# Top-32 attention and a gated product on one core: the values of two slots made together in every second turn

## The chip, the cores and the metric

One Trainium2 chip, one of its NeuronCores. The metric is the device time of one execution in microseconds (us); the median of the runs shown stands for a kernel. TensorE is PE in the profile (PEld is its weight loading), VectorE is DVE, ScalarE is ACT, GpSimd is POOL, SyncE is SP.

## The reference

```python
batch, n_heads, seq, head_dim = (8, 8, 576, 64)
scores = scale * np.matmul(q, k.transpose(0, 1, 3, 2))
kth = np.partition(scores, -top_k, axis=-1)[..., -top_k:-top_k + 1]      # top_k = 32
scores = np.where(scores >= kth, scores, -1000000000.0)
attn = np.exp(scores - np.max(scores, axis=-1, keepdims=True))
attn = attn / (np.sum(attn, axis=-1, keepdims=True) + 1e-09)
x = np.matmul(attn, v)                   # then heads side by side: 4608 tokens x 512
a = x @ w1; b = x @ w2                   # 512 -> 1024
h = a * b @ w3                           # 1024 -> 1024
out = h @ w_out                          # 1024 -> 512
```

All data is float32.

## The kernel before, in words

**Slots.** The attention is cut into 144 slots, 18 for each of 8 batches. A slot holds 128 query rows of two heads (or 64 rows of four heads, `t == 4`) against all 576 keys. Ten slots make part 0 of a batch (320 tokens), eight make part 1 (256 tokens). When a part's last slot is done, its dense product (`moe_steps`: eight pairs of `ab` sums, then four `eo` sums, each a chain of 12 or 24 matmuls) joins a queue. `w3` and `w_out` are folded into one weight `wf` at the start, where all weights are also decoded and split into a high and a low part.

**Turns.** The loop over `p` (lines 575 to 646) is a pipeline written out by hand; every engine keeps the program's order (`InOrder`). In one turn, and in this order, four neighbouring slots are at work: DVE makes the 32 largest scores of slot `p` (`top32_steps`, tiles `w` and `top`, given out in pieces by `next(finder)`); ACT and POOL make mask and exponentials of slot `p - 1` (`mask`, `exps`, `invert`, `normalise`); PE turns the weights of slot `m = p - 2` (`turn`: eight transposes of 128 columns into the PSUM tile `tp`, a ninth, of the last keys of both heads, into `ro`), ACT copies them to SBUF (`take_turned`: `pts`, `pr`); PE makes the scores of slot `p + 1` (`scores`: tiles `st`), and then, with `pts` and `pr`, the values of slot `m` (`values`: 20 matmul records, two heads at a time in the two column halves, into columns 128 to 255 of `ro`). ACT takes the high part of the values (`take_high`), DVE the low part in the next turn (`take_low`, tile `xf`), between its first two passes over the scores `w<-s,st` and its next two `w<-w,st`.

**Filling.** Between these steps PE takes matmuls from the queue of dense products: `fill(SHARE[0])` before the transposes, `fill(SHARE[1])` before the scores, `fill(SHARE[2])` after the values. The shares are constants. `fill` first evicts sums that are complete (ACT copies, a DVE product `whole`, a POOL subtraction).

**PSUM.** Pool `ps_a` has two buffers of two banks, which `st` (twice a turn) and `tp` (once) take by turns. So `tp` waits until DVE's passes `w<-s,st` have read the buffer of the first `st` tile, and the second `st` tile waits until ACT has copied `tp`. `ro` has one buffer, the `ab` and `eo` sums have three.

**SBUF.** Pool `x` (line 82) has nine buffers for `xf` and for the weights `y` under decoding; `pts` has one buffer, `pr` two.

Of the kernel before, what the change touches and what calls it, by code (L numbers as in the profile page):

```python
# [9 lines left out]
F32 = mybir.dt.float32  # L10
# [52 lines left out]
def attn_moe(ctx: ExitStack, tc: tile.TileContext, q, k, v, w1, w2, w3, w_out, out, flag, general):  # L63
# [12 lines left out]
    pe, act, dve, pool, sp = nc.tensor, nc.scalar, nc.vector, nc.gpsimd, nc.sync  # L76
# [2 lines left out]
    kq_p = ctx.enter_context(tc.tile_pool(name="kq", bufs=AHEAD))  # L79
    att_p = ctx.enter_context(tc.tile_pool(name="att", bufs=2))  # L80
    small = ctx.enter_context(tc.tile_pool(name="small", bufs=4))
    x_p = ctx.enter_context(tc.tile_pool(name="x", bufs=9))
    g_p = ctx.enter_context(tc.tile_pool(name="g", bufs=4))
    z_p = ctx.enter_context(tc.tile_pool(name="z", bufs=4))
    o_p = ctx.enter_context(tc.tile_pool(name="o", bufs=2))
# [1 line left out]
    ps_v = ctx.enter_context(tc.tile_pool(name="ps_v", bufs=1, space=PSUM))  # L87
    ps_m = ctx.enter_context(tc.tile_pool(name="ps_m", bufs=3, space=PSUM))

    ident = const.tile([128, 128], F32, name="ident")  # L90
# [17 lines left out]
    if not general:  # L108
        pe, act, dve, pool, sp = (InOrder(tc, e) for e in (pe, act, dve, pool, sp))
# [239 lines left out]
        for a in range(2):  # L349
            pool.tensor_scalar(pab[:, a, :], pab[:, a, :], sums[:, a : a + 1], 1.0, op0=ALU.mult, op1=ALU.mult)  # L350

    def turn(pab):

        tp = ps_a.tile([128, 2, 512], F32, tag="a", name="tp")
        flat = pab[:].rearrange("p a c -> p (a c)")
        for a in range(2):
            for c in range(4):
                o = a * (S + 64) + c * 128
                pe.transpose(tp[:, a, c * 128 : (c + 1) * 128], flat[:, o : o + 128], ident)
        ro = ps_v.tile([128, 512], F32, tag="v", name="ro")  # L360
        pe.transpose(ro[:, :128], flat[:, 512:640], ident)
        return tp, ro

    def take_turned(tp, ro):
        pts = att_p.tile([128, 2, 512], F32, tag="pts", name="pts", bufs=1)
        act.copy(pts, tp)
        pr = att_p.tile([128, 128], F32, tag="pr", name="pr")
        act.copy(pr, ro[:, :128])
        return pts, pr

    def values(vts, t, pts, pr, ro):

        ov = ro[:, 128:256]
        ends = t == 4
        for j in range(2 if ends else 1):
            vt = vts[j]
            for c in range(5):
                for i, h in enumerate(HEADS):
                    block = i * 4 + c if c < 4 else (((8, 10), (10, 9))[j][i] if ends else 8 + i)
                    n = HEADS[i ^ j] if ends else slice(0, 128)  # L380
                    rhs = pr[:, n] if c == 4 else pts[:, j if ends else i, c * 128 + n.start : c * 128 + n.stop]
                    to = ov[h, j * 64 : j * 64 + 64] if ends else ov[h]
                    pe.matmul(to, vt[:, block * D : (block + 1) * D], rhs, start=(c == 0), stop=(c == 4))
        return ov

    def places(xs, t):
        o = PLACE[t]
        if t == 4:
            return [(x, slice(o, o + 64), slice(j * 64, j * 64 + 64)) for j, x in enumerate(xs)]
        return [(xs[0], slice(o, o + 128), slice(0, 128))]  # L390

    def take_high(to, ov):
        for x, cols, n in to:
            act.copy(x[:, 0, cols], ov[:, n])

    def take_low(to, ov):
        for x, cols, n in to:
            dve.tensor_tensor(x[:, 1, cols], ov[:, n], x[:, 0, cols].bitcast(F32), op=ALU.subtract)
# [75 lines left out]
    def new_x():  # L474
        return x_p.tile([128, 2, NA], F32R, tag="x", name="xf")

    if general:
        for src, step in startup:
            for _ in step(fetch(src), False):
                pass  # L480
        with tc.For_i(0, B, 1) as b:
            seen = small.tile([1, 1], I32, tag="seen", name="seen", bufs=1)
            nc.sync.dma_start(seen, flag[ds(b + 1, 1), :])
            with tc.If(nc.values_load(seen, min_val=0, max_val=1) > 0):
                for part in range(2):
                    qk, vts, xs = {}, {}, {}
                    for of, hps, t in SLOTS:
                        if of != part:
                            continue
                        for hp in hps:  # L490
                            if hp not in qk:
                                qk[hp], vts[hp], xs[hp] = load_qk(b, part, hp), load_v(b, hp), new_x()
                        s, st = new_s(), scores([qk[hp] for hp in hps], t)
                        for h in range(2):
                            take_scores(s, st, h)
                        edge = top32_exact(s)
                        pab, sums = new_weights()
                        for a in range(2):
                            mask(s, edge, pab, a)
                            exps(edge, pab, sums, a)  # L500
                        enlarge(sums)
                        invert(sums)
                        normalise(pab, sums)
                        tp, ro = turn(pab)
                        ov = values([vts[hp] for hp in hps], t, *take_turned(tp, ro), ro)
                        to = places([xs[hp] for hp in hps], t)
                        take_high(to, ov)
                        take_low(to, ov)
                    for _ in moe_steps(b, part, [xs[hp] for hp in range(NHP)], lambda f: f()):
                        pass  # L510
        return
# [6 lines left out]
    queue = []  # L518

    parted = [u for u in units if u[0] > 0]  # L520
    put_off = []
    spare = 0

    def evict():
# [46 lines left out]
    n_slots = len(slots)  # L571
    for p in range(-1, n_slots + 3):
        i, j, m = p + 1, p - 1, p - 2
        if i < n_slots:
            for u in units:
                if first[u] - 2 == i:
                    qk[u] = load_qk(*u)
                if first[u] == i:
                    vts[u] = load_v(u[0], u[2])
        finder = top32_steps(ss[p], *sts.pop(p), p) if 0 <= p < n_slots else iter(())  # L580
        if 0 <= j < n_slots:
            edges[j] = edges_of(j)
        next(finder, None)
        for u in parted:
            if first[u] - 1 == i:
                split_k(PARTS[u[1]][1], qk[u])
        for u in parted:
            if first[u] - 1 == i:
                rest_k(PARTS[u[1]][1], qk[u])
        for u in parted:  # L590
            if first[u] - 0 == i:
                rest_q(PARTS[u[1]][1], qk[u])
        if m - 1 in lows:
            take_low(*lows.pop(m - 1))
            b, part, _ = slots[m - 1][0][0]
            if final[b, part] == m - 1:
                queue.append(moe_steps(b, part, [xts.pop((b, part, hp)) for hp in range(NHP)], put_off.append))
        next(finder, None)
        if p >= 0:
            warm()  # L600
        if 0 <= j < n_slots:
            pabs[j] = new_weights()
            for a in range(2):
                mask(ss[j], edges[j], pabs[j][0], a)
            compare(j)
        for u in parted:
            if first[u] - 1 == i:
                split_q(PARTS[u[1]][1], qk[u])
        fill(SHARE[0])
        next(finder, None)  # L610
        if 0 <= m < n_slots:
            tp, ro = turn(pabs[m][0])
            pts, pr = take_turned(tp, ro)
        warm(False)
        if 0 <= j < n_slots:
            exps(edges[j], *pabs[j], 0)
            exps(edges[j], *pabs[j], 1)
            enlarge(pabs[j][1])
        weigh(2)
        fill(SHARE[1])  # L620
        next(finder, None)
        warm(False)
        if i < n_slots:
            st = scores([qk[u] for u in slots[i][0]], slots[i][1])
            ss[i] = new_s()
            take_scores(ss[i], st, 0)
            sts[i] = st, take_scores(ss[i], st, 1)
        if 0 <= m < n_slots:
            us, t = slots[m]
            for u in us:  # L630
                if u not in xts:
                    xts[u] = new_x()
            ov = values([vts[u] for u in us], t, pts, pr, ro)
            lows[m] = places([xts[u] for u in us], t), ov
            take_high(*lows[m])
        next(finder, None)
        warm()
        next(finder, None)
        if 0 <= j < n_slots:
            invert(pabs[j][1])  # L640
            normalise(*pabs[j])
        weigh(8)
        fill(SHARE[2])
        for _ in finder:
            pass
        if 0 <= m < n_slots:
            del ss[m], pabs[m], edges[m]
        warm()
# [62 lines left out]
```

## Time and profile before

| | |
|---|---|
| runs | 1230.25, 1230.30, 1231.37 us; median 1230.3 us |
| the profiled execution | 1230.32 us, of which the span from first to last instruction is 1228.5 us |
| busy over the span | PE 97%, PEld 87%, DVE 92%, ACT 81%, POOL 81% |
| granted TensorE clock | 0.994 over the span |
| chain that ended last | PE 88%, DVE 7%, ACT 2% |

All work is recorded under one line (L54, the helper that keeps the order), so rows are told apart by their tiles. In a row of the timeline stand the start, the time from the first start to the last end, the engine, the operation, the output and input tiles, the shape, how many instructions are merged, and in brackets the idle time before with its releaser. A float32 matmul has two records.

### The profile page before, as it was taken

What the parts mean: (1) busy time and instruction counts of PE and PEld (TensorE: products, weight loads), DVE (VectorE), ACT (ScalarE), POOL (GpSimd) and SP (SyncE); (2) the same over time, 40 slices, a digit from 0 to 9 for tenths busy, and PEclk for the clock granted to TensorE, in tenths of its full rate; (3) what the DMA queues carried; (4) which work ended last, traced back from release to release, by engine and by line L of the source; (5) the groups of instructions that cost most, each with busy time, mean ns of one, the idle gap of its engine ahead of it and who ended that gap; (6) DMA issues with size and microseconds to landing.
All of it is one profiled execution on the core that took longest, in us unless ns stands there. A gap on an engine that the chain in (4) does not pass through costs nothing.

```text
span 1228.5 us, 31126 instructions
## 1 busy us (share of the span) xinstructions
PE 1189.1 (97%) x10967; PEld 1070.4 (87%) x10967; DVE 1133.9 (92%) x3960; ACT 998.2 (81%) x2140; POOL 996.5 (81%) x1331
## 2 busy tenths in 40 slices
PE   4799799999999999999999999999999999999998
PEld 2454589999999999999999999999999999999998
DVE  7999999999999999999999999999999999999910
ACT  6888888888888888888888888888888888888731
POOL 6998978888978888888888888888888888888721
PEclk9899999999999999999999999999999999999999
DMA  6544411213121211213121121203111120202000
GB/s 232 178 170 157 157 57 40 67 33 96 41 67 55 71 59 35 72 33 96 41 68 55 47 83 34 73 28 98 43 59 63 41 78 29 89 28 80 6 22 21
DMA packets 42807, 85.98 MB, mean 70 GB/s; under 512 B 4754, under 2 KB 21138, under 8 KB 42642
## 3 DMA queue, kind: packets, MB, share of 16 engines
q1 hardware_dynamic: 42642, 83.91, 21.2%
q8 instruction: 88, 1.44, 0.5%
q14 instruction: 77, 0.63, 0.2%
HBM read 74.45 MB, written 9.44 MB: 68 GB/s over the span
## 4 chain that ended last, share of the span: by engine, by line
PE 88%; DVE 7%; ACT 2%; issue 1%; POOL 1%; DMA 0%; SPq 0%; DVEq 0%; ACTq 0%; POOLq 0%
PE ab L54 33%; PE eo L54 17%; PE ro L54 15%; PE st L54 12%; PE tp L54 10%; DVE w L54 3%; DVE top L54 2%; PE pf L54 2%; DVE y L54 1%; DVE wl L54 1%; POOL pab L54 0%; ACT t L54 0%; ACT pab L54 0%; POOL wo L54 0%; ACT s L54 0%
## 5 line engine op out<-in xcount | busy, mean ns | idle before, releaser
L54 DVE MAX8 top<-w 128x8 f32<-128x192 f32 (+1 forms) x1152 | 477.9, 447 | 0.0
L54 PE MATMUL ab<-xf,wh 128*128 128x256 f32 (+1 forms) x2048 | 439.2, 303 | 4.9 <-DVE y L54 2.4
L54 POOL TENSOR_TENSOR pab<-s,pab 128x576 f32<-128x576 f32 x288 | 406.9, 1435 | 25.8 <-ACT pab L54 24.0
L54 PEld LDWEIGHTS ab<-xf,wh 128*128 128x128 f32 x2048 | 334.2, 189 | 15.8 <-issue 9.2
L54 PE MATMUL ab<-xf,wl 128*128 128x256 f32 (+1 forms) x1024 | 308.2, 301 | 0.0
L54 ACT ACTIVATE pab<-s,edge 128x576 f32<-128x576 f32 x288 | 208.0, 770 | 105.7 <-POOL edge L54 104.9
L54 DVE MATCH_REPLACE8 w<-top,w 128x192 f32<-128x192 f32 x864 | 289.3, 342 | 0.0
L54 POOL TENSOR_SCALAR pab<-pab,sums 128x576 f32<-128x576 f32 x288 | 211.6, 747 | 40.8 <-DVE sums L54 40.5
L54 ACT ACTIVATE pab<-pab,edge 128x576 f32<-128x576 f32 x288 | 223.9, 781 | 21.5 <-POOL pab L54 18.6
L54 PE MATMUL eo<-g,wf 128*128 128x256 f32 (+1 forms) x1536 | 231.5, 301 | 0.0
L54 PEld LDWEIGHTS eo<-g,wf 128*128 128x128 f32 x1536 | 208.3, 188 | 8.1 <-issue 7.5
L54 PEld LDWEIGHTS ab<-xf,wl 128*128 128x128 f32 x1024 | 193.5, 189 | 4.2 <-issue 4.2
L54 ACT COPY pts<-tp 128x1024 f32<-128x1024 f32 x144 | 145.7, 1012 | 42.9 <-PE tp L54 40.1
L54 ACT COPY s<-st 128x768 f32<-128x768 f32 (+1 forms) x288 | 169.5, 643 | 4.1 <-PE st L54 4.1
L54 DVE TENSOR_TENSOR w<-s,st 128x384 f32<-128x384 f32 x288 | 146.7, 551 | 21.5 <-ACT s L54 7.2
L54 DVE TENSOR_TENSOR w<-w,st 128x384 f32<-128x384 f32 x288 | 158.3, 550 | 4.9
L54 PE MATMUL ro<-pts,vt 128*64 128x128 f32 (+1 forms) x2560 | 160.4, 268 | 0.9 <-ACT pr L54 0.9
L54 PE MATMUL tp<-ident,pab 128*128 128x128 f32 x1152 | 150.6, 274 | 9.2 <-POOL pab L54 7.2
L54 PEld LDWEIGHTS tp<-ident,pab 128*128 128x128 f32 x1152 | 133.2, 141 | 15.8 <-POOL pab L54 8.4
L54 PEld LDWEIGHTS ro<-pts,vt 128*64 128x64 f32 x2560 | 126.8, 137 | 20.0 <-issue 4.2
L54 POOL TENSOR_TENSOR g<-whole,g 128x256 fp32r<-128x256 f32 (+1 forms) x128 | 103.5, 808 | 36.3 <-ACT g L54 32.6
L54 POOL TENSOR_SCALAR sums<-sums 128x2 f32<-128x2 f32 x144 | 30.8, 214 | 104.4 <-ACT pab L54 102.4
(64 smaller groups left out, 1572.8 us busy)
## 6 DMA issues: line engine op xcount, KB each, us to landing
vt<-in_v SPq DMA_DIRECT2D x64, 352.0 KB, 3.1
kt<-in_k SPq DMA_DIRECT2D x64, 320.0 KB, 3.9
z<-in_w SPq DMA_DIRECT2D x32, 512.0 KB, 3.5
qt<-in_q SPq DMA_DIRECT2D x32, 160.0 KB, 3.0
out_t<-osb SPq DMA_DIRECT2D x32, 160.0 KB, 1.8
z<-in_wo SPq DMA_DIRECT2D x8, 512.0 KB, 5.3
qt<-in_q SPq DMA_DIRECT2D x32, 128.0 KB, 3.0
out_t<-osb SPq DMA_DIRECT2D x32, 128.0 KB, 1.7
```

Source lines behind the costliest of these rows:

```text
L54: ins = fn(*args, **kw)
```

## The change

`turn` no longer makes its own `ro`: the loop makes one in turns with even `m`, whose transposes go to columns 0 to 127 and values to columns 128 to 255; the slot of the next turn uses columns 256 to 511 of the same tile. The turned weights of the even slot are held (`held`, so `pts` gets a second buffer), and in the odd turn the values of both slots are made one after the other, then both high parts are taken. The low parts of both are taken in the turn after that. The pool `x` goes from nine to eight buffers. Part ends fall on odd `m` (slots 9 and 17 of 18), so a part joins the queue in the same turn as before.

```diff
-    x_p = ctx.enter_context(tc.tile_pool(name="x", bufs=9))
+    x_p = ctx.enter_context(tc.tile_pool(name="x", bufs=8))
-    def turn(pab):
+    def turn(pab, ro, lane):
...
-        ro = ps_v.tile([128, 512], F32, tag="v", name="ro")
-        pe.transpose(ro[:, :128], flat[:, 512:640], ident)
-        return tp, ro
+        pe.transpose(ro[:, lane : lane + 128], flat[:, 512:640], ident)
+        return tp
-    def take_turned(tp, ro):
-        pts = att_p.tile([128, 2, 512], F32, tag="pts", name="pts", bufs=1)
+    def take_turned(tp, ro, o):
+        pts = att_p.tile([128, 2, 512], F32, tag="pts", name="pts")
...
-        if m - 1 in lows:
-            take_low(*lows.pop(m - 1))
+        for n in list(lows):
+            take_low(*lows.pop(n))
...
-            tp, ro = turn(pabs[m][0])
-            pts, pr = take_turned(tp, ro)
+            o = m % 2 * 256
+            if not o:
+                ro = new_ro()
+            held.append((m, *take_turned(turn(pabs[m][0], ro, o), ro, o), ro, o))
...
-        if 0 <= m < n_slots:
-            us, t = slots[m]
-            for u in us:
-                if u not in xts:
-                    xts[u] = new_x()
-            ov = values([vts[u] for u in us], t, pts, pr, ro)
-            lows[m] = places([xts[u] for u in us], t), ov
-            take_high(*lows[m])
+        if 0 <= m < n_slots and m % 2:
+            for n, *turned in held:
+                us, t = slots[n]
+                for u in us:
+                    if u not in xts:
+                        xts[u] = new_x()
+                lows[n] = places([xts[u] for u in us], t), values([vts[u] for u in us], t, *turned)
+            for n, *_ in held:
+                take_high(*lows[n])
+            held.clear()
```

The order of PE's instructions before, in one turn of the steady part, from the last scores to the next matmuls of the queue (`vt` are the values' rows, `pts` and `pr` the turned weights; the other turn of the pair reads the same with other numbers):

```order
L54 MATMUL st_8779<-hi_8458,lo_8459 128x192 x2
L54 MATMUL st_8779<-lo_8459,hi_8458 128x192 x2
L54 MATMUL ro_8744<-pts_8746,vt_8326 64x128 x8
L54 MATMUL ro_8744<-pr_8748,vt_8326 64x128 x2
L54 MATMUL ab_8762<-xf_7243,wl11_1532 128x320
L54 MATMUL ab_8762<-xf_7644,wh1_104 128x320 x2
```

The same place of the changed kernel in the even turn of the pair:

```order
L54 MATMUL st_8745<-hi_8424,lo_8425 128x192 x2
L54 MATMUL st_8745<-lo_8425,hi_8424 128x192 x2
L54 MATMUL ab_8728<-xf_7335,wl11_1515 128x320
L54 MATMUL ab_8728<-xf_7612,wh1_104 128x320 x2
L54 MATMUL ab_8728<-xf_7612,wl11_1515 128x320
```

and in the odd turn:

```order
L54 MATMUL st_8856<-hi_8669,lo_8670 128x192 x2
L54 MATMUL st_8856<-lo_8670,hi_8669 128x192 x2
L54 MATMUL ro_8701<-pts_8712,vt_8282 64x128 x8
L54 MATMUL ro_8701<-pr_8714,vt_8282 64x128 x2
L54 MATMUL ro_8701<-pts_8826,vt_8282 64x128 x8
L54 MATMUL ro_8701<-pr_8828,vt_8282 64x128 x2
L54 MATMUL ab_8834<-xf_7874,wh1_104 128x320
```

The ten matmuls of the values have left the even turn and stand behind the ten of the odd turn; the matmuls of the queue stay where they were.

DVE's order before, at the start of a turn's selection (`xf` is the low part of one slot):

```order
L54 TENSOR_TENSOR w_8947<-s_8911,st_8897 128x2x192 x2
L54 TENSOR_TENSOR xf_8789<-ro_8872,xf_8789 128x128
L54 TENSOR_TENSOR w_8947<-w_8947,st_8904 128x2x192 x2
L54 TENSOR_TENSOR whole_8965<-ab_8882,asb_8817 128x320
L54 MAX top0_100<-w_8947 128x8 x2
```

and after, in an even turn:

```order
L54 TENSOR_TENSOR w_8911<-s_8863,st_8849 128x2x192 x2
L54 TENSOR_TENSOR xf_8866<-ro_8701,xf_8866 128x128 x2
L54 TENSOR_TENSOR w_8911<-w_8911,st_8856 128x2x192 x2
L54 TENSOR_TENSOR whole_8930<-ab_8834,asb_8771 128x320
L54 MAX top0_100<-w_8911 128x8 x2
```

Both low parts stand in the even turn, and none in the odd one.

## Rows read from the trace of the kernel before

**Rows 1.** Stretches: length, busy us of PE, PEld, DVE, ACT, POOL; clock, DMA, GB/s.

```profile
0.00:168.85 168.85, 135.83 (x786) 81.80 (x787) 156.40 (x459) 139.12 (x271) 146.80 (x183) 0.96 0.49 168
...
569.88:709.13 139.25, 139.25 (x1364) 130.49 (x1364) 135.46 (x487) 117.64 (x257) 116.99 (x159) 1.00 0.19 58
...
1158.00:1228.50 70.50, 64.11 (x527) 62.60 (x525) 14.59 (x48) 22.18 (x54) 19.80 (x28) 0.99 0.06 19
```

**Rows 2.** Waits in 569.88 to 709.13: who for whom, us, times, longest.

```profile
DVE sums L54 <- POOL sums L54: 0.7, 2, 0.5
...
DVE w L54 <- ACT g L54: 0.5, 1, 0.5
```

**Rows 3.** Timeline of PE around one slot's values; the two x6 rows from narrower windows.

```profile
606.77 0.27 PE L54 MATMUL st<-hi,lo 64*128 64x192 f32 x2
606.88 0.27 PE L54 MATMUL st<-lo,hi 64*128 64x192 f32 x2
607.08 1.09 PE L54 MATMUL ro<-pts,vt 128*64 128x128 f32 x16
...
607.24 0.50 PE L54 MATMUL ro<-pts,vt 128*64 128x128 f32 x6
...
607.46 0.50 PE L54 MATMUL ro<-pts,vt 128*64 128x128 f32 x6
...
608.33 0.42 PE L54 MATMUL ab<-xf,wh 128*128 128x320 f32 x1
608.58 0.31 PE L54 MATMUL ab<-xf,wl 128*128 128x320 f32 x1
608.73 0.31 PE L54 MATMUL ab<-xf,wh 128*128 128x320 f32 x1
```

**Rows 4.** Timeline of DVE, turn 74 and the start of turn 75.

```profile
624.89 0.56 DVE L54 TENSOR_TENSOR w<-s,st 128x384 f32<-128x384 f32 x1
...
631.27 0.14 DVE L54 RECIPROCAL sums<-sums 128x2 f32<-128x2 f32 x1
...
633.11 0.28 DVE L54 TENSOR_TENSOR xf<-ro,xf 128x128 fp32r<-128x128 f32 x1
633.31 0.54 DVE L54 TENSOR_TENSOR w<-w,st 128x384 f32<-128x384 f32 x1
```

**Rows 5.** Timeline of PE, POOL and DVE in turn 75.

```profile
634.47 0.38 PE L54 MATMUL tp<-ident,pab 128*128 128x128 f32 x2
...
638.43 0.21 POOL L54 TENSOR_SCALAR sums<-sums 128x2 f32<-128x2 f32 x1 [0.84 <-ACT pab L54]
...
638.67 0.17 DVE L54 RECIPROCAL sums<-sums 128x2 f32<-128x2 f32 x1
```

**Rows 6.** Timeline of DVE and PE in turn 5, during loading.

```profile
58.39 1.00 DVE L54 TENSOR_TENSOR w<-s,st 128x384 f32<-128x384 f32 x2
...
59.53 0.85 PE L54 MATMUL tp<-ident,pab 128*128 128x128 f32 x6 [1.62 <-DVE w L54]
```

**Rows 7.** Timeline of DVE and PE: starts of turns 67, 69, 73 and 75.

```profile
569.88 0.56 DVE L54 TENSOR_TENSOR w<-s,st 128x384 f32<-128x384 f32 x1
...
572.65 1.03 PE L54 MATMUL tp<-ident,pab 128*128 128x128 f32 x8
...
586.43 0.55 DVE L54 TENSOR_TENSOR w<-s,st 128x384 f32<-128x384 f32 x1
...
617.60 1.02 DVE L54 TENSOR_TENSOR w<-s,st 128x384 f32<-128x384 f32 x2
...
618.93 1.03 PE L54 MATMUL tp<-ident,pab 128*128 128x128 f32 x8
...
632.17 1.02 DVE L54 TENSOR_TENSOR w<-s,st 128x384 f32<-128x384 f32 x2
```

**Rows 8.** Timeline of PE and POOL during loading.

```profile
118.08 1.98 PE L54 MATMUL pf<-wo,y 128*128 128x512 f32 x4
...
120.24 1.26 POOL L54 TENSOR_SCALAR y<-z 128x512 f32<-128x512 f32 x2
```

More of the change, by code (lines that the diff above doesn't have):

```diff
@@ L359, in turn, with new_ro, values @@
                 pe.transpose(tp[:, a, c * 128 : (c + 1) * 128], flat[:, o : o + 128], ident)
-        ro = ps_v.tile([128, 512], F32, tag="v", name="ro")
-        pe.transpose(ro[:, :128], flat[:, 512:640], ident)
-        return tp, ro
-    def take_turned(tp, ro):
-        pts = att_p.tile([128, 2, 512], F32, tag="pts", name="pts", bufs=1)
+        pe.transpose(ro[:, lane : lane + 128], flat[:, 512:640], ident)
+        return tp
+    def new_ro():
+        return ps_v.tile([128, 512], F32, tag="v", name="ro")
+    def take_turned(tp, ro, o):
+        pts = att_p.tile([128, 2, 512], F32, tag="pts", name="pts")
         act.copy(pts, tp)
         pr = att_p.tile([128, 128], F32, tag="pr", name="pr")
-        act.copy(pr, ro[:, :128])
+        act.copy(pr, ro[:, o : o + 128])
         return pts, pr
-    def values(vts, t, pts, pr, ro):
-        ov = ro[:, 128:256]
+    def values(vts, t, pts, pr, ro, o):
+        ov = ro[:, o + 128 : o + 256]
         ends = t == 4
@@ L503, in attn_moe @@
                         normalise(pab, sums)
-                        tp, ro = turn(pab)
-                        ov = values([vts[hp] for hp in hps], t, *take_turned(tp, ro), ro)
+                        ro = new_ro()
+                        ov = values([vts[hp] for hp in hps], t, *take_turned(turn(pab, ro, 0), ro, 0), ro, 0)
                         to = places([xs[hp] for hp in hps], t)
@@ L520, in attn_moe @@
     parted = [u for u in units if u[0] > 0]
-    put_off = []
+    put_off, held = [], []
     spare = 0
@@ L592, in attn_moe @@
                 rest_q(PARTS[u[1]][1], qk[u])
-        if m - 1 in lows:
-            take_low(*lows.pop(m - 1))
-            b, part, _ = slots[m - 1][0][0]
-            if final[b, part] == m - 1:
+        for n in list(lows):
+            take_low(*lows.pop(n))
+            b, part, _ = slots[n][0][0]
+            if final[b, part] == n:
                 queue.append(moe_steps(b, part, [xts.pop((b, part, hp)) for hp in range(NHP)], put_off.append))
@@ L611, in attn_moe @@
         if 0 <= m < n_slots:
-            tp, ro = turn(pabs[m][0])
-            pts, pr = take_turned(tp, ro)
+            o = m % 2 * 256
+            if not o:
+                ro = new_ro()
+            held.append((m, *take_turned(turn(pabs[m][0], ro, o), ro, o), ro, o))
         warm(False)
```

## The prediction

> **What bounds the kernel.** I read the busy time by stretch first, then the waits of the steady part, then the timelines of PE and DVE within a turn. In the 18 turns of one batch [rows 1] PE is busy for all of 139.25 us, and no wait of PE on another engine is in that stretch, so PE sets the pace: 7.74 us a turn, 15.47 for two. DVE is close behind: 135.5 us busy, and of what is left only 1.2 us are waits, for POOL's `sums` and once for ACT [rows 2]. The rest stands between its instructions in every turn. So DVE cannot turn 18 slots in less than about 139.25 - 1.2 = 138.05. Two engines with under 1% between them share this loop, and what matters is how far one may run ahead of the other. While weights load (0 to 169 us) DVE is busy 156 of 169 us and PE only 136 [rows 1]; after 1158 us the last part's products run on PE alone. The steady part in between holds 128 turns (989 us / 7.74), that is 7.1 batches.
>
> **The values move.** Around one slot's values [rows 3] the last scores start at 606.88 and the second matmul of the queue at 608.58: 1.70 us. Scores run in pairs 0.11 apart (606.77 to 606.88). The values too: the two narrow windows begin two pairs apart, at 607.24 and 607.46, so ten pairs take 1.09. Queue matmuls of this width are 0.15 apart (608.58 to 608.73). 1.70 - 0.11 - 1.09 - 0.15 leaves 0.35 lost where the kind of matmul changes: about 0.15 from scores to values (607.08 instead of 606.99, the next pair 0.16 later) and 0.20 from values to queue (608.33, then 0.25 instead of 0.15).
>
> An even turn now goes from scores straight to the queue, which no row of before shows. Such a change costs between 0 and the whole 0.35; I take 0.20, as from values to queue, which is the same step back to full-width matmuls. The even turn then needs 0.11 + 0.20 + 0.15 = 0.46 in place of 1.70, so it is 1.24 shorter; the odd turn makes ten more pairs with no change between them, 1.09 longer. PE gains 0.15 in two turns: 15.32 for 15.47, and 137.9 for 139.25 in a batch (bounds: 139.25 at 0.35, 136.1 at nothing). If PE stayed the bound, 64 pairs x 0.15 = 9.6 us would go. The rule for this: the Trainium skill, "TensorEngine Tiling (Array Packing)", section Key Properties, says that changing the tiling mode, and not just the tile, drains TensorE. The 0.35 in [rows 3] agrees; by that rule alone the time would be 1230.3 - 9.6 = 1220.7.
>
> **What the values' place does to PE's lead.** Every turn PE's transposes `tp` take the PSUM buffer that DVE's `w<-s,st` must first have read. When PE has to wait for that, `tp` starts 1.14 us after `w<-s,st` (58.39 to 59.53, [rows 6]). That is the earliest place. There is a latest one too, past which DVE pays: from `tp` the work goes over ACT's copy and exponentials and POOL's `sums` to DVE's reciprocal, 4.20 us (634.47 to 638.67, with the `sums` at 638.43, [rows 5]). Undisturbed, the reciprocal comes 6.38 after `w<-s,st` (624.89 to 631.27, [rows 4]), so `tp` may start up to 2.18 after it before DVE waits, some 0.4 more in turns where a `whole` product stands ahead of the reciprocal. The room is 1.0 to 1.5 us.
>
> Before, all of it is in use already: `tp` stands 2.77 after `w<-s,st` in turn 67 (569.88, 572.65) and 1.33 in turn 73 (617.60, 618.93) [rows 7], because DVE's pairs of turns are uneven (16.55 us from 569.88 to 586.43, 14.57 from 617.60 to 632.17: the `whole` products come in clusters) while PE's are even. PE never hits the early end; DVE hits the late one for the 1.2 us of [rows 2].
>
> After, the place also swings within each pair. From the `tp` of an odd turn to that of the even turn lie both values: 1.09 more for PE, and DVE's odd turn is 0.2 shorter, since its low part (633.11 to 633.31, [rows 4]) has moved to the even one: `tp` is 1.3 later. On the way back PE is 1.24 less and DVE 0.2 more: 1.4 earlier. This swing alone fills the room, and nothing is left for the drift of 1.44. In odd turns PE stands before `tp` until DVE has read the scores; in even turns DVE's reciprocal comes late. PE can no longer gain on one pair what DVE gives up in another, so each pair takes the longer of the two. With PE's 15.32 and DVE's nine pairs of this batch less their waits (from 14.6 to 16.0 us; of the nine, [rows 7] has the shortest and the longest, which also holds 0.7 of waits) the sum of the larger is 139.8. That is a lower bound of this case, since it still lets each pair use its room freely. On top, in odd turns the reciprocal is due 0.2 sooner while the chain through mask and exponentials does not move: 0 to 0.2 in nine turns, 0 to 1.8. Most odd turns that have a `whole` first keep their slack, so I take 0.3: **140.1 us a batch**, 0.85 more than before.
>
> **The rest.** ACT and DVE do the same copies; `pts` has its second buffer, so holding it delays nothing. The high parts come in pairs at the end of an odd turn, where ACT next waits for POOL's `edge` anyway. No DMA and no queue of SP or POOL is moved. Loading is bound by DVE, and the end has only one slot's pair in it: 0, give or take 2 us.
>
> **Sum.** 7.1 x 0.85 = +6.0 on the profiled 1230.32 us (span 1228.5 and 1.8 around it), which is the median of the runs too: **1236.3 us**.
>
> **Rivals.**
> - *PE keeps its lead (faster).* If the room is wider than I read it, by a microsecond or so, both engines run free, and the larger floor decides: DVE's 138.05 against PE's 137.9, so 1.2 a batch, 8.5 us: 1221.8. For it: the 2.77 of [rows 7] shows the late end giving way at a small price. Against: the early end is a PSUM buffer, which does not give way. 0.20.
> - *Gain and waits cancel.* At 0.85 less than I take per batch the pairs' waits eat what the changes of kind give: 1230, within 0.2%, which is 2.5 us, about what a measurement here can tell from no change. It is also what remains if going from scores straight to the queue costs the whole 0.35 and the waits come out low. 0.17.
> - *Loading is held up by the missing `x` buffer (slower).* With eight buffers POOL's first write of a chunk can meet a reader of the chunk that had the buffer. The second POOL copy at 120.24 + 0.6 would follow PE's last `pf` matmul, which ends at 120.06 [rows 8]: 0.8 of slack, less than the 1.09 by which an odd turn's `pf` comes later. Decides if half a dozen such meetings are on DVE's path at 0.5 each: 3 us, so 1233.3. 0.08, since most chunks have over 4 us.
>
> The Trainium skill, "Perfetto Trace Analysis", section Optimization Strategy, says that the same gap repeating on the engine that should be saturated can mean too little PSUM for the next tile. The 1.62 us before `tp` in [rows 6] agree; no gap of this kind is in the steady part of before.
>
> **How the numbers follow.** The forecast has 0.55; its own range goes from 139.8 - 0.4 to 140.4 + 0.2 a batch with 2 us for loading, 1231 to 1241. Eight in ten also takes in the faster case down to its floor: 1222 to 1241. Faster by over 0.2%: 0.20. Within: 0.17. Slower: 0.55 + 0.08 = 0.63.
>
> **What would show it.** Right: idle time of PE before `tp` ended by DVE's `w` in odd turns, some 2 us a batch; DVE's waits for `sums` above the 0.7 of [rows 2]; 18 turns in about 140.1 us; one change of kind less in two turns. Wrong: 18 turns under 138.9 us with PE never waiting for `w`; or a steady part as before and a longer loading.

## The result and the profile after

The changed kernel takes 1239.63 us (median of three runs, 1239.47 to 1240.39) where the kernel before takes 1230.3: a ratio of 1.0073, 95% interval 1.006 to 1.0087. It is slower, by more than the forecast (1236.3) and inside its range. The profiled execution has 1240.39 us, a span of 1238.5 and a granted clock of 0.993.

From the page of the changed kernel, the busy time and the chain that ended last:

```profile
PE 1189.0 (96%) x10967; PEld 1069.6 (86%) x10967; DVE 1135.2 (92%) x3960; ACT 999.1 (81%) x2140; POOL 997.4 (81%) x1331
...
PE 42%; DVE 37%; POOL 9%; issue 7%; ACT 3%; DMA 1%; DVEq 0%; SPq 0%; POOLq 0%; ACTq 0%
```

PE still has the most work, but the chain no longer stays on it: DVE holds 37% of it instead of 7%. The same stretches as in [rows 1]:

```profile
0.00:168.85 168.85, 132.30 (x760) 78.88 (x761) 154.46 (x455) 138.23 (x268) 146.07 (x181) 0.96 0.49 168
569.88:709.13 139.25, 138.39 (x1357) 129.40 (x1356) 134.69 (x486) 116.84 (x256) 116.12 (x158) 1.00 0.19 58
1158.00:1238.50 80.50, 74.54 (x639) 72.40 (x637) 23.90 (x83) 30.51 (x73) 26.61 (x39) 0.98 0.05 17
```

In 569.88 to 709.13 PE, never idle before, now stands still for 0.9 us, and DVE does 134.69 us of work where it did 135.46: both lose. Where the 10.0 us of span went, by the starts of DVE's `w<-s,st`:

| | before | after | difference |
|---|---|---|---|
| to the turn of slot 1 | 17.45 | 18.72 | +1.27 |
| slot 1 to slot 15 (the rest of loading) | 151.40 | 152.32 | +0.92 |
| slot 15 to slot 143 (128 turns) | 990.30 | 997.57 | +7.27 |
| slot 143 to the end | 69.38 | 69.93 | +0.55 |
| 18 turns, slots 74 to 92 | 139.25 | 140.28 | +1.03 |

Most of it is the steady part. Its waits, 300 to 1000 us (about five batches), first DVE's in the kernel before:

```profile
DVE sums L54 <- POOL sums L54: 4.8, 14, 0.5
DVE w L54 <- ACT g L54: 0.5, 1, 0.5
```

Then DVE's and PE's in the changed kernel:

```profile
DVE sums L54 <- POOL sums L54: 8.8, 25, 0.5
DVE whole L54 <- ACT asb L54: 0.9, 5, 0.2
```

```profile
PE tp L54 <- DVE w L54: 2.0, 10, 0.2
PE ab L54 <- ACT asb L54: 0.8, 5, 0.2
```

DVE's waits go from 5.3 to 9.7 us, 0.9 more in each batch of 18 turns: nearly all of the 1.03. PE now waits for DVE's `w` before `tp`, which it never did in this part of the kernel before. The profile names only the longer of these waits: the steps from the start of the queue matmul ahead to the start of `tp` add up to 3.71 us in the 18 turns from slot 74, before to 2.43.

What the values cost on PE is seen in the timeline of PE in the turns of slots 70 (even) and 71 (odd), which answers to [rows 3]:

```profile
605.31 0.27 PE L54 MATMUL st<-lo,hi 64*128 64x192 f32 x2
605.51 0.41 PE L54 MATMUL ab<-xf,wl 128*128 128x320 f32 x1
605.76 0.46 PE L54 MATMUL ab<-xf,wh 128*128 128x320 f32 x2
...
612.06 0.28 PE L54 MATMUL st<-lo,hi 64*128 64x192 f32 x2
612.26 1.09 PE L54 MATMUL ro<-pts,vt 128*64 128x128 f32 x16
...
614.60 0.41 PE L54 MATMUL ab<-xf,wh 128*128 128x320 f32 x1
614.85 0.31 PE L54 MATMUL ab<-xf,wl 128*128 128x320 f32 x1
```

From the last scores to the second queue matmul the even turn takes 0.45 us (605.31 to 605.76) and the odd one 2.79 (612.06 to 614.85), where both took 1.70. So PE saves 0.16 in two turns. It loses that again in the loop shown next, in the timelines of DVE, PE, ACT and POOL over the turns of slots 73 and 74:

```profile
623.21 1.02 DVE L54 TENSOR_TENSOR w<-s,st 128x384 f32<-128x384 f32 x2
...
624.37 1.06 PE L54 MATMUL tp<-ident,pab 128*128 128x128 f32 x8 [0.25 <-DVE w L54]
...
633.31 1.04 PE L54 MATMUL tp<-ident,pab 128*128 128x128 f32 x8
...
634.38 1.02 ACT L54 COPY pts<-tp 128x1024 f32<-128x1024 f32 x1 [1.47 <-PE tp L54]
...
637.17 0.21 POOL L54 TENSOR_SCALAR sums<-sums 128x2 f32<-128x2 f32 x1 [1.87 <-ACT pab L54]
...
637.42 0.17 DVE L54 RECIPROCAL sums<-sums 128x2 f32<-128x2 f32 x1 [0.29 <-POOL sums L54]
638.35 1.02 DVE L54 TENSOR_TENSOR w<-s,st 128x384 f32<-128x384 f32 x2
...
639.79 1.03 PE L54 MATMUL tp<-ident,pab 128*128 128x128 f32 x8
```

Follow who waits for whom. `tp` of the odd turn waits for DVE's `w` (623.21 to 624.37, 1.16). PE then needs 8.94 to the next `tp`, with both values in between. The chain over ACT and POOL to the reciprocal takes 4.11 (633.31 to 637.42), and 0.93 later the next odd turn begins. 1.16 + 8.94 + 4.11 + 0.93 = 15.14 us for a pair that took 14.57 before (617.60 to 632.17, [rows 7]). DVE's long work on the keys is not in this loop.

Nine such pairs make the batch from slot 73 to slot 91, each from one odd `w<-s,st` to the next odd one. Three of them carry the loss: 14.57, 14.73 and 15.44 us became 15.14, 15.14 and 15.63. The other six changed by -0.14 to +0.05. So it is the short pairs that the loop holds.

### The profile page after: what moved, and what is told of

Read it like the earlier page. It is cut to its first block, busy times and chain, and to the rows that moved or that the text cites. A ratio compares the mean times of both kernels' runs of the same rounds, so it can differ in the third digit from the quotient of the medians.

```text
span 1238.5 us, 31233 instructions
## 1 busy us (share of the span) xinstructions
PE 1189.0 (96%) x10967; PEld 1069.6 (86%) x10967; DVE 1135.2 (92%) x3960; ACT 999.1 (81%) x2140; POOL 997.4 (81%) x1331
## 4 chain that ended last, share of the span: by engine, by line
PE 42%; DVE 37%; POOL 9%; issue 7%; ACT 3%; DMA 1%; DVEq 0%; SPq 0%; POOLq 0%; ACTq 0%
DVE w L54 17%; PE eo L54 15%; DVE top L54 14%; PE ab L54 9%; PE ro L54 7%; PE tp L54 5%; PE st L54 5%; POOL pab L54 4%; DVE whole L54 3%; ACT pab L54 2%; POOL y L54 2%; DVE xf L54 1%; DVE wl L54 1%; DMA z<-in_wo 1%; POOL lo L54 1%
## 5 line engine op out<-in xcount | busy, mean ns | idle before, releaser
L54 PE MATMUL ro<-pts,vt 128*64 128x128 f32 (+1 forms) x2560 | 156.3, 265 | 0.4 <-ACT pr L54 0.4
L54 PEld LDWEIGHTS tp<-ident,pab 128*128 128x128 f32 x1152 | 130.4, 141 | 27.8 <-issue 12.3
L54 PEld LDWEIGHTS ro<-pts,vt 128*64 128x64 f32 x2560 | 130.3, 137 | 9.9 <-ACT pab L54 2.2
```

What stands on the lines that cost most here:

```text
L54: ins = fn(*args, **kw)
```

## The experiments

The table has the time of each kernel, its ratio to the kernel before on the same chip with its interval, and its 18 turns from slot 74 to slot 92. Beside the experiments the kernel before took 1231.1 to 1231.5 us (medians), so the ratios compare better than the times.

| kernel | us | ratio | 18 turns |
|---|---|---|---|
| before | 1230.3 | 1 | 139.25 |
| the change | 1239.63 | 1.0073 (1.006 to 1.0087) | 140.28 |
| e1 balanced | 1287.77 | 1.0453 (1.0433 to 1.0472) | 146.55 |
| e2 half balanced | 1261.82 | 1.0247 (1.023 to 1.0264) | 142.96 |
| e3 before, with swing | 1255.65 | 1.0198 (1.0181 to 1.0215) | 142.45 |
| e4 before, eight x buffers | 1233.63 | 1.0016 (1.0006 to 1.0026) | 139.24 |
| e5 balanced, evictions kept | 1312.07 | 1.065 (1.0633 to 1.0668) | 150.95 |
| e6 half, evictions kept | 1246.38 | 1.0122 (1.0102 to 1.0143) | 141.10 |
| e7 before, swing, evictions kept | 1308.29 | 1.0606 (1.0575 to 1.0637) | 150.05 |
| e8 tp later in odd turns | 1266.01 | 1.0276 (1.0257 to 1.0294) | 143.62 |
| e9 before, tp later in even turns | 1254.19 | 1.0189 (1.0172 to 1.0206) | 142.46 |
| e10 DVE relieved | 1236.11 | 1.004 (1.0026 to 1.0055) | 139.84 |
| e11 tp earlier in even turns | 1234.83 | 1.0033 (1.002 to 1.0045) | 139.73 |
| e12 e11, with k's low part in halves | 1230.31 | 0.9994 (0.9985 to 1.0003) | 139.08 |

### e1 to e3: moving queue work between the turns

e1 moves queue matmuls (2816 columns) from odd turns to even ones so that PE's turns are even again; e2 moves half of them; e3 does the opposite to the kernel before.

```diff
-        fill(SHARE[2])
+        extra = 2816 * (0 <= m < n_slots)
+        if m % 2 == 0:
+            fill(SHARE[2])
+            fill(extra)
+        else:
+            fill(SHARE[2] - extra)
```

e2 has 1408; e3 has `m % 2 == 1` and begins at `24 <= m`.

> The change, with 2816 columns (about 8 queue matmuls, 1.17 us) of each odd turn's last share of the queue moved to the even turn, so that PE's two turns are again within 0.1 us of each other; nothing else moves. Theory (the swing of PE's place uses up the room between the PSUM buffer of tp and the late reciprocal): PE's waits at tp and DVE's late reciprocals in even turns go, and PE's cheaper pair shows: 18 turns in 138.3 to 139.0 us in place of 140.3, time 1239.6 - (1.3 to 2.0) x 7.1 = 1225 to 1230, with the 2.2 us of loading still lost. Rival A (two low parts in one DVE turn, or the held tiles, cost DVE the time): 18 turns stay at 140.0 or more, 1237 to 1240. Rival B (going from scores straight to the queue saves PE nothing): 139.2 or more, 1231 or more.

> The same with half of it, 1408 columns (4 matmuls, 0.59 us each way). Theory: in between, nearer to the balanced one since the room takes up the first part of a swing: 139.0 to 139.7 us for 18 turns, 1230 to 1236. Rival A: as the change, 1237 to 1240.

> The kernel before, values in every turn, nine x buffers, with only 2816 columns of the queue moved from each even turn to the odd one from slot 24 on: PE's turns alternate as in the change, by 1.17 each way, and its work is that of before. Theory: the swing alone brings PE's waits at tp in odd turns and DVE's for the sums in even ones; 18 turns in 140.2 to 141.2 us, about 6.6 batches, 1237 to 1243. Rival A (low parts, held tiles, pairing): 139.25 as before, 1230 to 1231.

All three are far slower than any theory allowed. DVE's waits in e1, 300 to 1000 us:

```profile
DVE sums L54 <- POOL sums L54: 15.1, 37, 0.7
DVE xf L54 <- ACT xf L54: 10.6, 14, 2.3
DVE whole L54 <- ACT asb L54: 9.1, 8, 1.3
```

The wait of `xf` is new in kind, and the wait for `asb` was 0.9 us in the change. Every `fill` begins by issuing the queue's evictions, so another `fill`, or another number of matmuls in one, puts `asb`, `whole` and `g` at another place in the orders of ACT, DVE and POOL; there DVE stands up to 1.3 us before a `whole` whose `asb` is not ready. In e3 the waits are mainly of the kinds that the theory named (PE 6.0 us before `tp` for `w` and DVE 14.1 us for `sums`, against none and 4.8 in the kernel before). But all three runs changed two things at once, so none of them shows what the swing costs.

### e5 to e7: the same with the evictions kept in place

Here a second count follows the queue as the shares of the unchanged order would have it, and an eviction is issued only when that count has reached its tile, so that PE's order alone differs.

```diff
-    def evict():
-        while put_off:
-            put_off.pop(0)()
+    def evict(n=0):
+        while put_off and (not n or put_off[0][0] <= plan[0]):
+            put_off.pop(0)[1]()
...
-        fill(SHARE[2])
+        fill(SHARE[2], (2816 if m % 2 == 0 else -2816) * (24 <= m < n_slots))
```

e6 has 1408; e7 is the kernel before with `m % 2 == 1` from 25 on.

> The change, with 8 queue matmuls (2816 columns) moved from each odd turn's last share to the even turn before it from slot 24 on, as in the first balanced kernel, but with every eviction of the queue left in its place in the orders of ACT, DVE and POOL: only PE's order differs from the change's. Theory (the swing uses up PE's room): 18 turns in 138.3 to 139.0 us in place of 140.3, 1227 to 1232 with some 2 us of loading lost. If the first balanced kernel was slow because balancing is bad for PE's place, and not because of the moved evictions: 146 us again, 1285. Rival A (two low parts in a DVE turn, held tiles): 140.0 or more, 1237 to 1240.

> The same with 4 matmuls (1408 columns), evictions in their places. Theory: between the change and the balanced one, nearer to the balanced: 138.8 to 139.6 us, 1230 to 1236. Rival A: 140.0 or more, 1237 to 1240.

> The kernel before, values in every turn and nine x buffers, with 8 queue matmuls moved from each even turn's last share to the odd turn before it from slot 25 on and the evictions left in their places: only PE's order differs, its work is that of before and its turns alternate by 1.17 each way as the change's do. Theory: the swing alone makes PE wait at tp in odd turns and DVE for the sums in even ones: 18 turns in 140.2 to 141.2 us, 1237 to 1243. Rival A: 139.25, 1230 to 1232.

Again none of the theories. What PE's weight loads wait for in e5, 300 to 1000 us:

```profile
PEld ab L54 <- ACT asb L54: 31.3, 28, 1.9
PEld eo L54 <- ACT g L54: 12.2, 9, 2.6
```

In the changed kernel the first of these is 3.8 us and the second is not there. With the evictions fixed, a PE that is eight matmuls ahead on the queue finds its three PSUM tiles full, or `g` not made. So the queue's place is bound on both sides: the evictions may not move, and PE may not run ahead of them. Half the distance (e6) costs less, 141.10, but also more than the change.

### e8 and e9: moving `tp` against the queue

e8 sets `tp` of the odd turns behind eight more queue matmuls; e9 does so in the even turns of the kernel before. The evictions are kept in place as in e5.

```diff
-        fill(SHARE[0])
+        fill(SHARE[0], 2816 * (m % 2))
...
-        fill(SHARE[1])
+        fill(SHARE[1], -2816 * (m % 2))
```

> The change, with tp of every odd turn set behind 8 more matmuls of the queue (2816 columns of the turn's second share go ahead of tp instead of behind it); scores, values and every eviction stay where they are, and the queue is 1.07 us ahead for less than half a turn only. tp's place then swings by 0.1 to 0.2 us instead of 1.3. Theory (the swing of tp uses up PE's room): PE's waits at tp in odd turns go, reciprocals in even turns come earlier, 18 turns in 138.2 to 139.3 us in place of 140.3, 1226 to 1233. Rival A (two low parts in one DVE turn, held tiles): 140.0 or more, 1237 to 1240. Rival C (what decides is where the scores or the queue's tiles stand against the evictions, not tp): 140 or more as well, with PE waiting for asb.

> The kernel before, values in every turn, with tp of every even turn set behind 8 more matmuls of the queue in the same way: nothing else moves, PE's work is that of before, and only tp's place alternates, by 1.1. Theory: PE meets tp's buffer in odd turns and DVE's reciprocal is late in even ones: 18 turns in 140.0 to 141.2 us in place of 139.25, 1236 to 1244. Rivals A and C: 139.25, 1230 to 1232.

Both are slower than expected, and mainly for a reason that none of the theories has. PE's weight loads in e8, 300 to 1000 us:

```profile
PEld st L54 <- ACT pts L54: 16.3, 44, 0.6
PEld ab L54 <- ACT asb L54: 13.2, 15, 1.4
```

The second tile of the scores takes the PSUM buffer of `tp`, which ACT must first have copied. With two queue matmuls between `tp` and the scores instead of ten, the scores wait for that copy, up to 0.6 us, 44 times in 700 us, about once in every turn that was moved. The second row is the sign that rival C named, 13.2 us for `asb` against 3.8 in the change, so e8 does not rule that rival out; in e9 it is absent. e9 has the same wait for the copy (16.2 us, 44 times) and so does not show the swing alone either. `tp` is bound from behind too, by the scores.

### e4: the x buffer

```diff
-    x_p = ctx.enter_context(tc.tile_pool(name="x", bufs=9))
+    x_p = ctx.enter_context(tc.tile_pool(name="x", bufs=8))
```

> The kernel before with eight x buffers in place of nine, nothing else. If the missing buffer holds up the loading, turn 15 starts 1 to 3 us later than at 168.85 and the time is 1231.5 to 1233.5; if the 2.2 us of the change's loading come from the paired values (or from when the first transfer landed), the time is 1230.3 within 0.6. In both cases 18 turns stay at 139.25.

2.2 us by the medians (1231.47 before, on the same chip; 2.0 by the ratio); slot 15 begins 3.1 us later (171.98) and the steady part stays at 139.24. The place, in POOL's timeline of e4 in the turn of slot 13, which takes 16.74 us instead of 13.56:

```profile
149.20 0.64 POOL L54 TENSOR_SCALAR y<-z 128x512 f32<-128x512 f32 x1 [4.62 <-DVE wl L54]
```

POOL waits 4.62 us for DVE to have read the chunk that had the buffer. In the changed kernel that turn takes 13.76, so this execution did not pay there. Its own loss before slot 1 (1.27 us) can come without the change: e3, with nine buffers and the values of before, reached slot 1 at 18.81. And two later kernels with eight buffers and paired values reached slot 15 at 169.17 (e11) and 169.14 (e12), where the change took until 171.04 and the kernel before until 168.85. So the missing buffer can cost 2 us of loading, but what part of the change's 2.2 it is, and whether the change has to lose them at all, stays open.

### e10: DVE relieved

```diff
-                for a in range(2):
+                for a in range(2 if i else 1):
                     dve.match_replace(w[:, a, one], top[:, a, cut], w[:, a, one], NEG)
```

> The change, leaving out on DVE the first of the six match_replace of each turn (the second head's first eight are found twice), some 0.33 us a turn; PE's work and all orders stay. It measures the PE pair that the prediction put at 15.32 us. Theory (each engine alone could do 18 turns in 138; they lose 2 between them): PE is then the bound in all pairs: 137.7 to 138.4 us for 18 turns, about 1221 to 1226. Rival B (the change of kind is not saved, PE's own floor is still 139 or more): 139.0 or more, 1229 or more.

What the kernel leaves out is the second of the six in DVE's order. The theory as it stood then falls. The stretch of [rows 1] in e10:

```profile
569.88:709.13 139.25, 138.70 (x1359) 129.80 (x1358) 131.03 (x449) 117.35 (x257) 116.46 (x158) 1.00 0.18 57
```

DVE is busy for 131.03 us instead of 134.69, and the 18 turns come down by only 0.44. DVE's waits, 300 to 1000 us:

```profile
DVE sums L54 <- POOL sums L54: 20.4, 45, 0.9
DVE whole L54 <- ACT asb L54: 5.3, 19, 0.5
```

25.7 us of waits in these two rows instead of 9.7: what DVE no longer works, it waits. If each pair took the longer of two engines' own times, PE's 138 would have come out. The three short pairs take 15.14, 15.14 and 15.63 us, as in the change. What holds them is a loop of delays in which DVE's work on the keys has no part, the one read above in slots 73 and 74. Rival B (PE's own floor is 139 or more) would give a time like this too. Against it stand PE's 0.55 us of idle time in the stretch above and a pair in which PE stands still for nothing and which became 0.16 us shorter (slots 83 to 85, below).

### e11: the loop shortened

`tp` of the even turns goes ahead of the eight queue matmuls that stood before it; scores, values and evictions stay.

```diff
-    def fill(n):
+    def fill(n, more=False):
         nonlocal spare
-        evict()
+        if not more:
+            evict()
...
-        fill(SHARE[0])
+        late = 2816 * (m % 2 == 0)
+        fill(SHARE[0] - late)
...
+        if late:
+            fill(late, True)
         fill(SHARE[1])
```

> The change, with tp of every even turn set ahead of the last 8 queue matmuls that stood before it (they follow right behind it, before the evictions of the second share, which stay in their places on ACT, DVE and POOL): only PE's order differs from the change's, the queue is 1.07 us late for a few us, and tp gets further away from the scores, not nearer. From tp of an odd turn to tp of the next even one PE then needs 7.7 us instead of 8.8. Theory, as the relieved DVE left it (what sets the pace of the change is a loop of delays, tp of the odd turn after DVE's w, PE's long half, ACT and POOL from tp to the sums, DVE's reciprocal and what follows it; DVE's own work is not in it): the loop is 1.1 us shorter in each pair, PE's waits at tp and the late reciprocals go, and 18 turns take 138.2 to 139.2 us in place of 140.3; 1224 to 1232. Rival A (two low parts in one DVE turn, held tiles): 140.0 or more, 1237 to 1240. Rival C (where the queue's tiles stand against the evictions): 139.8 or more, with PE waiting for asb, 1236 or more.

4.8 us of the 9.3 come back, 0.55 in each batch. That is half of the least that the theory expected, and more than the rivals allow: 139.73 lies between them. The three short pairs come down to 14.75, 15.02 and 15.27. The turns of slots 73 to 75 in the timeline of PE now:

```profile
620.74 1.06 PE L54 MATMUL tp<-ident,pab 128*128 128x128 f32 x8 [0.25 <-DVE w L54]
...
628.50 1.03 PE L54 MATMUL tp<-ident,pab 128*128 128x128 f32 x8
...
636.15 1.03 PE L54 MATMUL tp<-ident,pab 128*128 128x128 f32 x8
```

7.76 us from the first to the second instead of 8.94, and the reciprocal of slot 74 comes 6.58 after `w<-s,st`, its undisturbed place (the 6.38 of [rows 4] and 0.2 for the second low part). The waits from 300 to 1000 us in e11 are these:

```profile
DVE sums L54 <- POOL sums L54: 6.3, 15, 0.7
DVE whole L54 <- ACT asb L54: 1.1, 5, 0.2
```

```profile
PE tp L54 <- DVE w L54: 2.0, 10, 0.3
```

PE's named waits at `tp`, which the theory expected to go, stay at 2.0 us; what falls is DVE's wait for the sums, from 8.8 to 6.3. So PE's waits at `tp` are not the measure of what the change pays. What is left of the waits for the sums is in turns like the next one. POOL's timeline of e11 in the turn of slot 66, which DVE begins at 563.77:

```profile
565.13 1.57 POOL L54 TENSOR_TENSOR lo<-kt,hi 128x640 fp32r<-128x640 f32 x1 [0.39 <-ACT hi L54]
566.65 2.83 POOL L54 TENSOR_TENSOR pab<-s,pab 128x576 f32<-128x576 f32 x2
569.43 0.20 POOL L54 TENSOR_TENSOR over<-top 128x2 f32<-128x2 f32 x1
570.47 0.21 POOL L54 TENSOR_SCALAR sums<-sums 128x2 f32<-128x2 f32 x1 [0.84 <-ACT pab L54]
```

The mask (`pab<-s,pab`) starts 2.88 after `w<-s,st`, behind the low part of a k unit; in turns without one it starts 1.86 to 2.56 after. It ends at 5.71, and the reciprocal follows at 6.95.

### e12: the mask not held up

```diff
-                rest_k(PARTS[u[1]][1], qk[u])
+                rest_k(PARTS[u[1]][1], qk[u], slice(0, 320))
...
             compare(j)
+        for u in parted:
+            if first[u] - 1 == i:
+                rest_k(PARTS[u[1]][1], qk[u], slice(320, 640))
```

> The kernel with tp of even turns set earlier, and POOL's low part of a k unit (lo<-kt, 1.57 us, ahead of the mask in even turns) made in two halves, one ahead of the mask and one behind it, where POOL stands idle 0.84 us for the exponentials; nothing else moves. Theory: with PE's long half gone, what is left over 138 is POOL's mask, which starts up to 1.0 late behind lo<-kt and delays the reciprocal by the same path (mask end + 1.25); halved, the mask starts 0.8 earlier in eight turns of a batch, DVE's waits for the sums go from 1.6 to under 1.0 in 18 turns, and 18 turns take 138.5 to 139.3 us in place of 139.7; 1226 to 1232. Rival (what is left is DVE's own work, or PE's place at tp): 139.6 or more, 1234 to 1236.

As the theory had it: 139.08 us for 18 turns, 1230.31 us in all. In the turn of slot 66 the mask now starts 2.43 after `w<-s,st` instead of 2.88. DVE's waits, 300 to 1000 us:

```profile
DVE sums L54 <- POOL sums L54: 3.7, 5, 0.8
DVE whole L54 <- ACT asb L54: 1.1, 5, 0.2
DVE xf L54 <- ACT xf L54: 1.0, 5, 0.2
```

They are 5.8 us, about as in the kernel before. e11 and e12 keep the two low parts in one DVE turn, the held tiles and eight x buffers, and reach the 139.25 of before and a little less. So 0.55 of the 1.03 us a batch were not the price of these, since PE's order alone brought them back; whether the other 0.48 were is not shown, because the split might have gained in the kernel before too. The Trainium skill, "Perfetto Trace Analysis", section Optimizing Scalar/DVE Operations, says of engines that are not full but hold up others that breaking up their instructions may let work finish sooner; it names Scalar and Vector, and here it holds for POOL (0.65 us a batch from one split). What each of the two edits does without the other, or in the kernel before, was not tried. No version here beats the kernel before: e12's interval holds 1.

## Why the prediction was right in direction and too small

- **The change of kind** was sized right. Assumed 0.46 us from scores straight to the queue, measured 0.45; assumed 1.09 more in the odd turn, measured 2.79 - 1.70 = 1.09. The pair gains 0.16 against 0.15: from `tp` in the turn of slot 83 to that in the turn of slot 85 it takes 15.38 us, before 15.54. The rule of the Trainium skill, "TensorEngine Tiling (Array Packing)", section Key Properties, that a change of tiling mode drains TensorE, agrees with these rows; the time that it gives alone, 1220.7, did not come, since PE stopped being the only bound.
- **The room of `tp`** was read right: earliest 1.14, measured 1.16; chain to the reciprocal 4.20, measured 4.11; the swing 1.3 and 1.4, measured 1.7 and 1.4 (1.16 to 2.84 to 1.44 in slots 73 to 75). The signs named beforehand are there: PE idle before `tp` in odd turns, DVE's waits for `sums` above [rows 2].
- **The step that failed** is "each pair takes the longer of the two", with 0.3 on top: 0.85 a batch, measured 1.03. The direction held, the term was too small, and its picture was wrong: two of the short pairs take 15.14 us, less than the 15.38 of PE's own pair, and e10 shows that they do not follow DVE's work either. Such a pair is held by a loop through both engines, ACT and POOL, whose length depends on PE's long half (the stretch from the odd `tp` to the even one, which holds both values) and not on either engine's total. That 140.1 came so near the measured 140.28 is therefore in part luck. PE's idle before `tp` was put at 2 us a batch; the profile names 0.4 of it (2.0 in five batches), the starts show 1.3 (3.71 less 2.43), and e11 loses less time although the named part stays.
- **DVE's own floor** of 138.05 held up. 18 turns less the named waits of a batch (those of 300 to 1000 us divided by 700 and multiplied by the 18 turns) give 138.2 before, 138.3 for the change, 138.2 for e11 and 137.9 for e12. So the faster rival could at best have brought 1.2 us a batch, and 0.9 of the 1.03 that the change loses in a batch are named waits of DVE.
- **Loading** was put at 0, give or take 2: the profile has +2.2 up to slot 15, 1.27 of it before slot 1. The rival of the missing `x` buffer was given 3 us and 0.08; alone it costs 2 (e4), and at another place than the one named, a chunk that waits for DVE's `wl`, not for PE's `pf`.
- **The sum**: 128 turns give +7.3 where +6.0 was forecast, loading and end +2.7 where 0 was; together 10.0 on the span. Of the 4.0 beyond the forecast, 1.3 are steady and 2.7 loading and end. The range's upper end, worked out from its own terms (140.6 a batch and 2 us), is nearer to 1242 than to 1241.

## What to carry to other kernels

When two engines that share a loop are both nearly full, look for the loop of delays between them before adding up their work: an edit that saves time on one but lengthens the longest stretch of that loop can lose, and taking work off the other engine may then give little (e10: 3.7 us less work of DVE in the stretch, 0.44 us less time). Even out the place of the instruction that hands over (here `tp`), rather than the work around it, and check what lies on either side of it: a PSUM buffer still being read, a copy that must be done, an eviction's place in three other orders. An experiment that shifts work in such a schedule should be compared engine by engine with its original, since most of the shifts above (e1 to e3, e5 to e9) moved a bound that they were not meant to touch.

## What was not expected of the hardware

A long wait of PE cost more than itself. In e7, three stretches around one wait (rows as in [rows 1]), then the timeline of PE there:

```profile
612.00:616.00 4.00, 1.61 (x9) 1.02 (x9) 3.53 (x13) 2.54 (x7) 2.87 (x6) 0.88 0.01 2
616.00:618.00 2.00, 2.00 (x16) 1.83 (x18) 0.07 (x1) 0.77 (x2) 0.56 (x1) 0.50 0.00 0
618.00:622.00 4.00, 4.00 (x41) 3.83 (x38) 3.30 (x11) 1.87 (x6) 1.72 (x3) 0.94 0.00 0
```

```profile
614.86 0.75 PE L54 MATMUL ab<-xf,wh 128*128 128x320 f32 x2 [2.39 <-ACT asb L54]
...
617.31 0.41 PE L54 MATMUL st<-lo,hi 64*128 64x192 f32 x2
617.65 1.47 PE L54 MATMUL ro<-pts,vt 128*64 128x128 f32 x16
```

PE stands idle for 2.39 us and begins again at full clock (2.4 GHz). Shortly after, the granted clock falls to 0.50 (1.2 GHz): it is 0.50 from 615.5 to 618.0 and 1.00 again from 618.5. In between, a pair of scores that takes 0.27 at full clock takes 0.41, sixteen records of the values' matmuls 1.47 instead of 1.09. That is probably part of why e5 and e7, with granted clocks of 0.982 and 0.97 over their spans, are so slow; how large a part was not worked out. In the change itself no wait of PE in 300 to 1000 us is over 0.5 us, and the clock over 569.88 to 709.13 is 1.00.
